# Attention and a feed-forward layer in one kernel: sums of squares, weight scales and masks made by other engines, under a new order of steps

## Chip, cores and metric

One core of one Trainium2 chip runs the whole program. The metric is the device time of one execution in microseconds. TensorE does the matmuls, VectorE, ScalarE and GpSimd the element work, SyncE (SP) issues loads and transposing transfers. Every engine and every queue runs its own instructions in the order in which they were written, and waits for others by semaphores.

## What is computed

```
scores = scale * q @ k.T                       # 8 batches, 8 heads, 576 positions, head size 64
mask   = local (0 <= rel < 32) for heads 0-3;  strided (rel >= 0, same position mod 32) for heads 4-7
attn   = softmax(where(mask, scores, -1e9)) @ v
x      = attn, laid out as 4608 tokens x 512
h      = x @ w_in                              # 512 x 1024
solu   = h * softmax(h)
ln     = (solu - mean) / sqrt(var + 1e-6) * g_ln
out    = ln @ w_out                            # 1024 x 512
```

`w_in` and `w_out` arrive as 64-bit floats and are decoded on the chip.

## The kernel before

**Precision.** TensorE multiplies 16-bit floats. A 32-bit operand is split into a high part (a rounded copy, written by ScalarE) and a low part (the remainder, written by VectorE), and a product is made as three matmuls: high x high, high x low, low x high. So that the parts fit, each operand is scaled by a power of two taken from its sum of squares: `pow2_scale` (lines 320 to 351) adds the partial sums over the partitions with a matmul against ones (L330), takes half the exponent as the root (L340), and makes the scale and its reciprocal by three small VectorE steps (L343 to L346).

**Attention.** For each batch there are four units (`unit`, from line 460): two of the strided heads (6 and 5 blocks, called half 1 in the code) and two of the local heads. A unit fills its scores with the mask (for batch 0 a matmul with the unit matrix, L505, later a ScalarE copy, L496), adds q k (L514), takes the maximum (L522), subtracts it (for batch 0's units by a matmul, L527, with the exponent behind it, L531), sums (L532, L545), inverts the sum (L549, L550), and scales by it on GpSimd (L553). For batch 0 the result is turned by TensorE (L565) and scaled on the way back by ScalarE with `one`, the reciprocal of the value scale (L568); later batches are split and turned by a transposing transfer (L580). Then come the product with the values (L607), and the split of the result into the ring of tokens, `xs` for strided and `xl` for local heads: high part by ScalarE (L628), low part by VectorE (L629).

**Values.** `v_scale` (line 390) finds the scale of a batch's values. It squares them on ScalarE with an accumulator (L410, two instructions for a batch), sums, and makes the scale; `hscale` (L418) combines it with the scale of `w_in`. There is a second way in the code, for batches named in `V_PE`: TensorE multiplies the upper halves of the values with themselves in blocks of 128 columns, and VectorE takes the diagonal. `V_PE` is empty. `v_split` (line 437) splits the values of batches 1 to 7 into high and low (L443, L444) and has three transfers shift the local ones by 32 rows into `ve` (L457); for batch 0 TensorE makes the shifted copy in three pieces (`load_first_v`, L377 and L378).

**Weights.** `prep_w` (line 796) loads `w_in` in four chunks of 128 rows, decodes each (`decode`: ScalarE L787, GpSimd L792, VectorE L793), takes the diagonal of its gram (L806, L809), makes one scale for all four, and then splits each chunk (L814 on ScalarE, L815 on VectorE). `prep_o` does the like for `w_out`.

**Feed-forward.** `ff(n)` handles 128 tokens: 24 matmuls of 512 columns with `w_in` (L671 to L673), two maxima (L677), exponent (L681), product and sums (L683), mean and squares (L687, L688), norms on GpSimd, split (L728, L729), a transposing transfer, 24 matmuls with `w_out` (L745 to L747), and the store (L755).

**Masks** are one loaded array of 128 x 3 x 96 (L277), from which GpSimd makes a copy for the strided units (L266) and the local ones (L272 to L274).

**Order.** The kernel doesn't issue as it goes. `Plan.add` collects 1576 steps, each with its engine, a planned duration and what it reads and writes. `ORDER` is a written-out list of step numbers, and the steps are issued in it. Filler matmuls on ones (L257), 56 of them, keep TensorE running at the start: 12 at first, `WARM` = 16 pairs and, later, `LATE` = 6 pairs.

Of the kernel before, what the change touches and what calls it, by code (L numbers as in the profile page):

```python
# [9 lines left out]
BF16 = mybir.dt.bfloat16  # L10
# [3 lines left out]
ALU = mybir.AluOpType  # L14
# [5 lines left out]
STRIDE = 32  # L20
# [40 lines left out]
V_PE = ()  # L61
# [4 lines left out]
47 1 3-5 29 27 22 28 39 21 2 82 34 6-8 48 23 49 20 30-31 40 50 35 42 53 9-11 36 32 105-106 89 107-108 41 37 90 109 91  # L66
38 83 92 110 12 54 13 93 44 59-60 94 0 45 84-85 33 123 55 124 51 140 56 25 86 147 14 65 95 125 139 61 111 43 148 62
126-127 149 15 52 16 87 17 57 18 172 150 112 19 98 141 26 58 96 66-67 296 63 151 68 295 128 64 99 142 69-70 152 71-72
97 73 143-144 80 129 100 113 88 173 114 153 103 81 174 177 299 101 116 74 115 117 332 76 104 175 165 24 102 187 166 75
178 300-301 118 132 167 302 154 77 315 179 130 121 46 119 316 120 131 78 133 331 155 189 188 122 168 145 169 317 182  # L70
170 303 134 318 137 338 180 138 158 135 485 156 159 79 136 190 157 339 304 297 176 305-306 184 171 319 487 215 320 340
181 183 307 341 321 354 185 342 355 160 333 216-217 343-344 163 322 161 486 357 186 345 164 218-220 346 191-192 162
193 235 194 222 195 356 308 221 196 201 358 309 298 359 223 199 237 334 363 224 323 310 207 236 211 213 364 238-239
200 225 240 212 324 255 241 365 546 226-227 311 242 366 313 257 325 312 491 347 492 314 335 229 488 326 256 243 337
203 258-260 230 197 244 493 329 262 261 275 198 494 327 245 507 263 330 328 205 277 204 246 336 202 348 367 349 264
352 508 278 231 209 232 247 276 248 350 509 279 265 523 280 524 656 353 249 210 547 208 206 282 351 549 380 655 250
495 251 510 368 530 369 360 281 228 266 548 233 283 146 370 531 284 511 532 382 533 371 550 401 267 372 381 234 534
269 383 214 551 555 512 285 379 535 384 270 373 286 556 513 385 557 496-497 287 252 657 253 498 387 694 536 558 499
559 489 661 388 386 268 374 500 402-403 490 422 404 514 289 377 405 375 378 376 290 254 406 515 658 693 501 389 502
271 503 407 423 505 662 408 424 409 504 392 410 425-426 390 537 413 361 443 291 560 552 391 847 516 272 525 663 393  # L80
517 288 411 664 444 395 427 412 396 428-429 273 506 414 677 445 397 430 526 518 716 561 274 416 446-447 415 678 665
538 553 539 679 448 417 519 850 394 450 521 455 464 562 540 431 680 700 719 434 432 449 563 529 522 292 666 717 293
520 701 294 433 451 527 466 564 528 702 667 703 718 452 465 541 720 453 398 467 435 704 399 542 668 468 543 681 469
721 682 544 437 436 545 669 454 722-723 438 683-684 471 725 849 362 470 685 400 456-457 565 848 571 472 726 473-475
573 418 659 458 727 592 885 705 566 728 572 853-854 574 439 554 670 567 419 476 459 575 660 671 420 855 706 1017 729
569 576 707 477 568 570 577 593 695 578 594 856 886 421 869 696 579 672 580 857 908 595 673 870 613 708 440 674 698
# [80 lines left out]
def attn_solu_kernel(ctx: ExitStack, tc: tile.TileContext, qloc, qstr, kloc, kstr, vloc, vstr, w_in, w_out, g, masks, out):  # L167
# [780 lines left out]
```

## Time and profile before

| | |
|---|---|
| time, median of 3 runs | 483.84 us (481.33 to 484.36) |
| the profiled execution: time, span | 482.54 us, 480.6 us |
| TensorE busy | 467.7 us (97%) |
| ScalarE, VectorE, GpSimd busy | 350.2, 323.3, 175.8 us |
| loads, first 30 us | 366 GB/s |
| first feed-forward matmul starts at | 45.63 us |

The span goes from the first to the last instruction; the time of a run is longer by what lies around it. A wait is the idle time of an engine just before an instruction, put down to what ended it. An idle engine costs time only if it is the one that sets the end in that stretch.

### The profile page before, as it was taken

How to read it: one execution, taken by the hardware profiler on the slowest of the kernel's cores; microseconds unless marked ns; L12 is line 12 of the kernel's file. 1: busy time of each engine (PE TensorE's matmuls, PEld its weight loads, DVE VectorE, ACT ScalarE, POOL GpSimd, SP SyncE). 2: the span in 40 equal slices, each digit the busy share in tenths (PEclk: the TensorE clock that was granted, in tenths of full speed). 3: DMA queues.
4: the chain of work that ended last, by engine and by line, in shares of the span. 5: the costliest groups of instructions: out<-in, count | busy, mean ns of one | idle time of the engine just before them, and what ended most of it. 6: DMA issues, size and time to landing. Idle time of an engine off the chain costs nothing.

```text
span 480.6 us, 15173 instructions
## 1 busy us (share of the span) xinstructions
PE 467.7 (97%) x6484; PEld 238.9 (50%) x6484; DVE 323.3 (67%) x699; ACT 350.2 (73%) x569; POOL 175.8 (37%) x328
## 2 busy tenths in 40 slices
PE   9988899999899999999999999999999999999997
PEld 3765455554455454545554454455454445444444
DVE  1599999989759867878686667655754764435440
ACT  3499999999787996787798677966664664564661
POOL 4533525476333423152414413422331723112420
PEclk9989999999999999999999999999999999999999
DMA  8997699698959997697759945575651794233353
GB/s 335 420 369 287 203 195 303 150 157 201 208 136 284 185 223 187 114 263 117 181 191 221 203 85 125 113 184 123 132 101 34 120 178 89 64 88 71 78 113 95
DMA packets 131555, 83.21 MB, mean 173 GB/s; under 512 B 117376, under 2 KB 118208, under 8 KB 130976
## 3 DMA queue, kind: packets, MB, share of 16 engines
q1 hardware_dynamic: 126304, 72.88, 65.2%
q10 hardware_dynamic: 5184, 9.37, 5.7%
q8 instruction: 50, 0.82, 0.7%
q14 instruction: 17, 0.14, 0.1%
HBM read 39.24 MB, written 9.44 MB: 101 GB/s over the span
## 4 chain that ended last, share of the span: by engine, by line
PE 85%; ACT 4%; DVE 4%; DMA 4%; issue 2%; SPq 1%; ACTq 0%; DVEq 0%
PE h_ps L671 12%; PE o_ps L745 11%; PE o_ps L746 11%; PE o_ps L747 11%; PE h_ps L672 11%; PE h_ps L673 11%; PE x_ps L607 4%; PE s_ps L514 4%; DMA ve<-vl 2%; PE o_ps L257 2%; DMA raw<-w_out 1%; ACT vs L410 1%; DVE st L677 1%; ACT raw L681 1%; DVE m L545 1%
## 5 line engine op out<-in xcount | busy, mean ns | idle before, releaser
L745 PE MATMUL o_ps<-ohi,cc 128*128 128x512 f16 x272 | 103.3, 380 | 0.0
L746 PE MATMUL o_ps<-obuf,cc 128*128 128x512 f16 x272 | 103.2, 379 | 0.0
L747 PE MATMUL o_ps<-ohi,cc 128*128 128x512 f16 x272 | 103.2, 379 | 0.0
L677 DVE TENSOR_REDUCE st<-h_ps 128x1 f32<-128x512 f32 x70 | 47.2, 686 | 50.6 <-PE h_ps L673 50.3
L683 DVE SCALAR_TENSOR_TENSOR raw<-h_ps,raw 128x512 f32<-128x512 f32 x70 | 47.4, 685 | 27.8 <-ACT raw L681 27.0
L681 ACT ACTIVATE raw<-h_ps,st,vsc 128x512 f32<-128x512 f32 x62 | 48.0, 775 | 24.8 <-DVE st L679 22.5
L553 POOL TENSOR_TENSOR t<-t,m 128x648 f32<-128x648 f32 (+5 forms) x32 | 40.9, 1279 | 64.7 <-DVE m L550 54.2
L729 DVE SCALAR_TENSOR_TENSOR cc<-raw,st,cc 128x1024 f16<-128x1024 f32 (+1 forms) x38 | 46.4, 1226 | 15.1 <-ACT cc L728 14.9
L671 PE MATMUL h_ps<-w,xl 128*128 128x512 f16 x140 | 53.3, 381 | 1.4 <-issue 0.9
L687 ACT ACTIVATE raw<-raw,st 128x1024 f32<-128x1024 f32 x36 | 41.2, 1147 | 17.5 <-DVE st L686 16.6
L671 PE MATMUL h_ps<-w,xs 128*128 128x512 f16 x140 | 53.1, 379 | 0.0
L672 PE MATMUL h_ps<-w,xs 128*128 128x512 f16 x140 | 53.1, 379 | 0.0
L673 PE MATMUL h_ps<-w,xs 128*128 128x512 f16 x140 | 53.1, 379 | 0.0
L673 PE MATMUL h_ps<-w,xl 128*128 128x512 f16 x140 | 53.1, 379 | 0.0
L672 PE MATMUL h_ps<-w,xl 128*128 128x512 f16 x140 | 53.1, 379 | 0.0
L728 ACT ACTIVATE cc<-raw,st 128x1024 f16<-128x1024 f32 (+1 forms) x38 | 41.6, 1100 | 13.1 <-POOL st L718 11.0
L747 PEld LDWEIGHTS <-cc 128*128 128x128 f16 x296 | 28.9, 98 | 33.6
L745 PEld LDWEIGHTS <-cc 128*128 128x128 f16 x296 | 28.9, 98 | 32.8 <-DMA cc<-cc 0.3
L746 PEld LDWEIGHTS <-cc 128*128 128x128 f16 x296 | 29.0, 98 | 31.8
L755 ACT ACTIVATE ob<-o_ps,st 128x512 f32<-128x512 f32 x34 | 23.3, 686 | 29.0 <-PE o_ps L747 25.9
L691 POOL TENSOR_SCALAR st<-st 128x1 f32<-128x1 f32 x36 | 14.9, 414 | 76.6 <-ACT raw L681 74.7
L716 POOL TENSOR_SCALAR st<-st 128x1 f32<-128x1 f32 x32 | 6.2, 194 | 97.6 <-ACT raw L688 96.8
(197 smaller groups left out, 889.8 us busy)
## 6 DMA issues: line engine op xcount, KB each, us to landing
out<-ob ACTq DMA_DIRECT2D x35, 256.0 KB, 2.3
q<-qstr SPq DMA_DIRECT2D x8, 594.0 KB, 5.3
k<-kstr SPq DMA_DIRECT2D x8, 594.0 KB, 5.5
q<-qloc SPq DMA_DIRECT2D x8, 576.0 KB, 5.2
k<-kloc SPq DMA_DIRECT2D x8, 576.0 KB, 5.3
raw<-w_in SPq DMA_DIRECT2D x4, 1024.0 KB, 15.3
ve<-vl SPq DMA_DIRECT2D x7, 480.0 KB, 5.5
vrs<-vstr SPq DMA_DIRECT2D x4, 768.0 KB, 6.4
```

Of the source, the lines that this page charges most:

```text
L671: nc.tensor.matmul(hv[i], xhi[cc], whi[:, cc, cols], start=(cc == 0), stop=False)
L672: nc.tensor.matmul(hv[i], xhi[cc], wlo[:, cc, cols], start=False, stop=False)
L673: nc.tensor.matmul(hv[i], xlo[cc], whi[:, cc, cols], start=False, stop=(cc == 3))
L677: add("dve", 0.69, lambda i=i: nc.vector.tensor_reduce((nm, nm2)[i], hv[i], axis=AX.X, op=ALU.max, negate=True), r=[HH[i]], w=[(ST, "nm", i)])
L681: add("act", 0.73, lambda i=i, q=q: nc.scalar.activation(e[:, parts2[i]], hv[i], AF.Exp, bias=nm, scale=hs, accum_out=q), r=[HH[i], (ST, " ...
L683: add("dve", 0.7, lambda i=i, x=x: nc.vector.scalar_tensor_tensor(u[:, parts2[i]], hv[i], 1.0, e[:, parts2[i]], op0=ALU.mult, op1=ALU.mult ...
L687: add("act", 1.13, lambda: nc.scalar.activation(u, u, AF.Identity, bias=mean), r=[(U, 0), (U, 1), (ST, "mean")], w=[(U, 0), (U, 1)])
L728: add("act", w / 1200 + 0.295, lambda cols=cols: nc.scalar.mul(c[:, 0, cols], u[:, cols], r), r=[(U, 0), (U, 1), (ST, "r")], w=CC[0][mine])
L729: add("dve", w / 980 + 0.23, lambda cols=cols: nc.vector.scalar_tensor_tensor(c[:, 1, cols], u[:, cols], r, c[:, 0, cols], op0=ALU.mult, o ...
L745: nc.tensor.matmul(dst, ct[:, cc, :], ohi[:, cc, cols], start=(cc == 0), stop=False)
L746: nc.tensor.matmul(dst, ct[:, cc, :], olo[:, cc, cols], start=False, stop=False)
L747: nc.tensor.matmul(dst, ct[:, 8 + cc, :], ohi[:, cc, cols], start=False, stop=(cc == 7))
```

## The change

Four things change, and the list of steps with them (1581 now).

`V_PE` is (0, 1): the values of batches 0 and 1 go by TensorE's grams, ten matmuls for the local and twelve for the strided values of each, instead of ScalarE's squares.

The input weights are scaled by halves: chunks 0 and 1 have one scale, 2 and 3 another (the rows of the first half meet the local heads, those of the second the strided heads). A step `common` takes the larger scale, and `rho` is each half's share of it. It goes into the value scales, one for each half of the heads (`hscale` has a third instruction), and for batch 0's strided units into the split of the result, whose low part is now one instruction for each block of a pair.

The masks are not loaded. GpSimd writes zeros and then affine selects put -8e9 where nothing may pass: four for the strided mask, ten for the local one.

The order is another throughout. At the start: SP loads q and local values before k, then chunks 2 and 1 of `w_in`, then q and k of the local heads, then chunks 0 and 3, then batch 0's strided values; batch 1's values come behind the second chunk of `w_out` (before, they came ahead of all of `w_out`). GpSimd makes the local mask, then the strided one, ahead of every decode. TensorE issues 22 fillers, one shifted piece, four fillers, both strided score products, and by the fourth gram of `w_in` 38 fillers and one batch's value grams (before, 44 fillers and two transposes). VectorE runs batch 0's value scale, both weight scales, `common` and `hscale` ahead of the first low part of the weights; ScalarE's first high part of the weights stands behind the first decode of `w_out`. Batch 0's last value product and unit 2 of batch 1 stand ahead of the first feed-forward matmul (before, the value product stood between the two halves of that tile).

```diff
-V_PE = ()
+V_PE = (0, 1)
...
-    vsc_sb = buf("vsc", [P, 6], n=4)
-    (mask_sb,) = buf("mask", [P, 3, KL])
+    vsc_sb = buf("vsc", [P, 8], n=4)
+    (mask_sb,) = buf("mask", [P, QS])
...
+    rho = w_sc[:, 10:12]
...
+    def keep(t, pattern, base, by):
+        nc.gpsimd.affine_select(out=t, in_=t, pattern=pattern, compare_op=ALU.is_ge, fill=-8e9, base=base, channel_multiplier=by)
     def mask_strided():
-        nc.gpsimd.tensor_copy(mk_str, mask_sb[:, 2:3, 0:QS].broadcast_to([P, 6, QS]))
+        nc.gpsimd.memset(mask_sb, 0.0)
+        for row in range(0, P, D):
+            m = mask_sb[row : row + D].rearrange("p (g j) -> p g j", j=NI)
+            keep(m, [[-NI, RS], [-1, NI]], 0, 1)
+            keep(m, [[NI, RS], [0, NI]], NI - 1, -1)
+        nc.gpsimd.tensor_copy(mk_str, mask_sb.unsqueeze(1).broadcast_to([P, 6, QS]))
     def mask_local():
-        m = mask_sb
+        near = mk_loc[:, 1, 0]
+        nc.gpsimd.memset(near, 0.0)
         for row in range(0, P, STRIDE):
...
+            keep(near[rows], [[1, KW]], -1, -1)
+            keep(near[rows], [[-1, KW]], STRIDE, 1)
+        nc.gpsimd.tensor_copy(mk_loc[:, 1, 1:6], mk_loc[:, 1, 0:1].broadcast_to([P, 5, KW]))
+        nc.gpsimd.tensor_copy(mk_loc[:, 0], mk_loc[:, 1])
+        for row in range(0, P, QL):
+            keep(mk_loc[row : row + STRIDE, 0, 0], [[1, KW]], -STRIDE, 0)
     def load_masks():
-        add("sp", 0.4, lambda: nc.sync.dma_start(mask_sb, masks), w=["mask_raw"])
...
         def hscale():
-            nc.vector.tensor_scalar(sc[:, 2:3], sc[:, 0:1], w_sc[:, 0:1], None, op0=ALU.mult)
+            nc.vector.tensor_scalar(sc[:, 2:3], sc[:, 0:1], w_sc[:, 8:9], None, op0=ALU.mult)
             nc.vector.reciprocal(sc[:, 4:5], sc[:, 2:3])
+            nc.vector.tensor_scalar(sc[:, 6:8], rho, sc[:, 1:2] if b else sc[:, 5:6], None, op0=ALU.mult)
...
-        add("act", w / 1266 + 0.354, lambda: nc.scalar.mul(hi, vr, sc[:, 1:2]), r=[("vr", a, raw), ("vsc", b % 4)], w=V[:1])
+        add("act", w / 1266 + 0.354, lambda: nc.scalar.mul(hi, vr, sc[:, 6 + a : 7 + a]), r=[("vr", a, raw), ("hsc", b % 4)], w=V[:1])
...
+            one, ONE = (vsc_sb[0][:, 5:6], "one") if half else (vsc_sb[0][:, 6:7], ("hsc", 0))
...
+            if b == 0 and half:
+                def low(src=src, dh=dh, dl=dl, k=k):
+                    for j in range(k):
+                        nc.vector.scalar_tensor_tensor(dl[:, j], src[:, j], rho[:, 1:2], dh[:, j], op0=ALU.mult, op1=ALU.subtract)
+                add("act", w / 1200 + 0.17, lambda src=src, dh=dh: nc.scalar.mul(dh, src, rho[:, 1:2]), r=[X[y], "w_sc"], w=H)
+                add("dve", w / 960 + 0.09 + 0.11 * k, low, r=[X[y], "w_sc", *H], w=L)
+                continue
...
-        for cc in range(4):
-            decode(stage[cc], ...)
+        for half in (0, 1):
+            mine = (2 * half, 2 * half + 1)
+            for cc in mine:
+                decode(stage[cc], ...)
...
-        pow2_scale(w_sc, [w_sc[:, 4 + cc : 5 + cc] for cc in range(4)], ...)
+            own = w_sc[:, 2 * half : 2 * half + 2]
+            pow2_scale(own, [w_sc[:, 4 + cc : 5 + cc] for cc in mine], ...)
...
+        def common():
+            nc.vector.tensor_scalar(w_sc[:, 8:9], w_sc[:, 0:1], w_sc[:, 2:3], None, op0=ALU.max)
+            nc.vector.reciprocal(w_sc[:, 9:10], w_sc[:, 8:9])
+            nc.vector.tensor_scalar(rho, w_sc[:, 0:4:2], w_sc[:, 9:10], None, op0=ALU.mult)
```

## Rows read from the trace of the kernel before

**Rows 1.** Page, busy time: engine, us, share of the span, instructions

```profile
PE 467.7 (97%) x6484; PEld 238.9 (50%) x6484; DVE 323.3 (67%) x699; ACT 350.2 (73%) x569; POOL 175.8 (37%) x328
```

**Rows 2.** Busy time by stretch: from:to, length, busy of each engine, clock, DMA, GB/s

```profile
0.00:30.00 30.00, 28.36 (x365) 16.04 (x366) 13.38 (x38) 14.83 (x22) 15.34 (x34) 1.00 0.92 366
30.00:60.00 30.00, 25.69 (x508) 16.73 (x508) 29.18 (x64) 29.06 (x47) 13.71 (x11) 0.94 0.76 280
60.00:100.00 40.00, 40.00 (x795) 21.17 (x794) 38.49 (x85) 39.51 (x66) 19.08 (x31) 1.00 0.86 207
```

**Rows 3.** Waits of TensorE: waiting <- releaser: us in total, times, longest

```profile
PE x_ps L607 <- DMA ve<-vl: 1.8, 1, 1.8
PE s_ps L514 <- ACT s_ps L496: 1.6, 2, 0.9
PE o_ps L330 <- DVE diag L834: 1.3, 1, 1.3
PE o_ps L257 <- DVE ones L253: 1.1, 1, 1.1
```

**Rows 4.** Busy time by stretch, the last 10.6 us

```profile
470.00:480.60 10.60, 7.05 (x57) 4.28 (x55) 0.35 (x1) 1.27 (x2) 0.00 (x0) 0.95 0.26 71
```

**Rows 5.** Busy time by stretch, of line L257 alone: matmul, weight load, clock, DMA

```profile
0.00:57.00 57.00, 15.82 (x56) 5.80 (x56) 0.97 0.84 333
```

**Rows 6.** Timeline, 14 to 56 us: start, length, engine, line, operation [wait before]

```profile
14.10 0.79 DVE L522 TENSOR_REDUCE m<-h_ps 128x5 f32<-128x270 f32 x2 [3.07 <-PE h_ps L514]
...
25.65 1.12 POOL L792 TENSOR_SCALAR raw<-raw 128x1024 int32<-128x1024 uint8 x1 [1.89 <-DMA raw<-w_in]
...
28.13 1.08 PE L806 MATMUL x_ps<-cc 128*128 128x128 bf16 x16
...
45.40 1.21 DVE L793 SCALAR_TENSOR_TENSOR obuf<-obuf,raw 128x1024 int32<-128x1024 int32 x1
...
45.63 0.38 PE L671 MATMUL h_ps<-w,xl 128*128 128x512 f16 x1
...
55.29 0.19 PE L330 MATMUL o_ps<-o_sc,ones 128*128 128x1 bf16 x2 [1.30 <-DVE diag L834]
```

**Rows 7.** Groups by line, ScalarE, 0 to 31 us: busy, mean ns | idle before

```profile
L410 ACT ACTIVATE vs<-vs 128x1536 f16<-128x1536 f32 x1 | 1.5, 1475 | 0.0
L410 ACT ACTIVATE vs<-vrl 128x1280 f16<-128x1280 f32 x1 | 1.3, 1262 | 0.0
L410 ACT ACTIVATION_READ_ACCUMULATOR vs<-vs 128x1 f32 x1 | 0.2, 193 | 0.0
```

**Rows 8.** Groups by line, VectorE, 27.1 to 46.62 us

```profile
L629 DVE TENSOR_TENSOR xs<-x_ps,xs 128x324 f16<-128x324 f32 (+1 forms) x4 | 1.8, 462 | 0.1
...
L809 DVE SCALAR_TENSOR_TENSOR diag<-x_ps,unit 128x128 bf16<-128x128 f32 x3 | 0.8, 271 | 0.3 <-PE x_ps L806 0.2
...
L809 DVE DVE_READ_ACCUMULATOR diag<-x_ps,unit 128x1 f32 x3 | 0.3, 84 | 0.0
...
L344 DVE RECIPROCAL w_sc<-w_sc 128x1 f32<-128x1 f32 x1 | 0.2, 165 | 0.0
...
L346 DVE TENSOR_SCALAR w_sc<-w_sc 128x1 f32<-128x1 f32 x1 | 0.2, 154 | 0.0
```

**Rows 9.** Busy time of TensorE by stretch, with the granted clock

```profile
30.00:32.00 2.00, 1.22 (x51) 1.00 1.04 422
32.00:34.00 2.00, 2.00 (x10) 0.58 1.01 410
34.00:36.00 2.00, 2.00 (x58) 0.56 1.04 422
```

**Rows 10.** Chain that ended last, in order of time: start, length, engine, line

```profile
7.68 0.86 PE x_ps L377 x2
8.54 0.97 PE x_ps L378 x2
```

**Rows 11.** Groups by line, GpSimd, 0 to 15 us

```profile
L273 POOL CAST mk_loc<-mask 32x384 bf16<-32x384 f32 x4 | 3.1, 770 | 0.0
L272 POOL CAST mk_loc<-mask 32x64 bf16<-32x64 f32 x4 | 0.9, 230 | 0.1
...
L315 POOL TENSOR_SCALAR_AFFINE_SELECT ident<-ident 128x128 f32<-128x128 f32 x1 | 0.3, 292 | 0.1
```

More of the change, by code (lines that the diff above doesn't have):

```diff
@@ L124 @@
+1550 1571 1575 1573-1574 1577 1579 1524 1580 1576 1578
 """
@@ L232, in attn_solu_kernel @@
     whi, wlo = w16[:, :, 0, :], w16[:, :, 1, :]
-    (w_sc,) = buf("w_sc", [P, 8])
+    (w_sc,) = buf("w_sc", [P, 12])
     (diag,) = buf("diag", [P, P], BF16)
@@ L799, in prep_w @@
         ST = [[("c", i, y, a) for y in range(2) for a in range(2)] for i in range(2)] + CT[:2]
-        for cc in range(4):
-            decode(stage[cc], w_in[cc * P : (cc + 1) * P, :].rearrange("p (a f) -> p a f", a=2), cc, ST[cc], ROOMS[cc], W_SHIFT)
-            def gram(cc=cc):
-                x = stage[cc].bitcast(BF16).rearrange("p (f t) -> p f t", t=2)[:, :, 1]
-                for i in range(8):
-                    nc.tensor.matmul(wg_ps[cc], x[:, i * P : i * P + P], x[:, i * P : i * P + P], start=(i == 0), stop=(i == 7))
-            add("pe", 0.6, gram, r=ST[cc], w=[("x", cc % 2)])
-            add("dve", 0.3, lambda cc=cc: nc.vector.scalar_tensor_tensor(diag, wg_ps[cc], 1.0, unit_sb, op0=ALU.mult, op1=ALU.mult, accum_out=w_sc[:, 4 + cc : 5 + cc]),
-                r=[("x", cc % 2), "unit"], w=[("wm", cc)])
@@ L812, in prep_w, with gram @@
[L812 to L817 removed]
+        for half in (0, 1):
+            mine = (2 * half, 2 * half + 1)
+            for cc in mine:
+                decode(stage[cc], w_in[cc * P : (cc + 1) * P, :].rearrange("p (a f) -> p a f", a=2), cc, ST[cc], ROOMS[cc], W_SHIFT)
+                def gram(cc=cc):
+                    x = stage[cc].bitcast(BF16).rearrange("p (f t) -> p f t", t=2)[:, :, 1]
+                    for i in range(8):
+                        nc.tensor.matmul(wg_ps[cc], x[:, i * P : i * P + P], x[:, i * P : i * P + P], start=(i == 0), stop=(i == 7))
+                add("pe", 0.6, gram, r=ST[cc], w=[("x", cc % 2)])
+                add("dve", 0.3, lambda cc=cc: nc.vector.scalar_tensor_tensor(diag, wg_ps[cc], 1.0, unit_sb, op0=ALU.mult, op1=ALU.mult, accum_out=w_sc[:, 4 + cc : 5 + cc]),
+                    r=[("x", cc % 2), "unit"], w=[("wm", cc)])
+            own = w_sc[:, 2 * half : 2 * half + 2]
+            pow2_scale(own, [w_sc[:, 4 + cc : 5 + cc] for cc in mine], [("wm", cc) for cc in mine], ("w_sc", half), (wg_ps[mine[1]][:, 0:1], ("x", 1)), mul=2.0**W_SHIFT, shift=0, floor=2.0**-64)
+            for cc in mine:
+                add("act", 1.13, lambda cc=cc, own=own: nc.scalar.mul(whi[:, cc], stage[cc], own[:, 1:2]), r=[("w_sc", half), *ST[cc]], w=[("wh", cc)])
+                add("dve", 1.28, lambda cc=cc, own=own: nc.vector.scalar_tensor_tensor(wlo[:, cc], stage[cc], own[:, 1:2], whi[:, cc], op0=ALU.mult, op1=ALU.subtract),
+                    r=[("w_sc", half), ("wh", cc), *ST[cc]], w=[("w", cc)], lock=True)
```

141 lines of the change are left out of this document (66 added, 75 removed).

## The prediction

> **What bounds the kernel now.** I read the page's engine table first, then busy time by stretch, then TensorE's waits, and only then the timeline of the first 60 us. TensorE is busy 467.7 of 480.6 us [rows 1], so 12.9 us of the span are not matmul. By stretch [rows 2] TensorE is filled without a gap from 60 to 100 us, while from 30 to 60 us VectorE (29.18 of 30) and ScalarE (29.06) are the full ones and TensorE is not: the start is bounded by the vector engines, the rest by TensorE. The listed waits [rows 3] put 1.8 us on one late copy of shifted values near 131 us, 1.6 us on mask copies, 1.3 us on the output weights' scale, 1.1 us on the very first memset; the others are under 1 us each. After the last matmul 10.60 - 7.05 = 3.55 us of store are left [rows 4]. So the memset and the store (4.65 us) stay whatever the order is, and 8.2 us of waits can be changed. In the first 57 us TensorE also runs 56 filler matmuls, 15.8 us busy [rows 5]; the change keeps all 56, since WARM and LATE stand.
>
> **The change part by part.** The profiled execution took 482.54 us for a span of 480.6, so 1.9 us lie around the span; the median of the runs is 483.84, 1.3 us above it. I sum against 480.6.
>
> TensorE. Two batches' values are squared by grams: (10 + 12) x 2 = 44 matmuls of 128x128, priced by the 16 grams of the input weights that took 1.08 us [rows 6], so 0.065 us each, 2.8 us in all with one more scale product. Nothing leaves TensorE. The span can therefore not fall below 467.7 + 2.8 + 4.65 = 475.2, a time of 477.1, and only if every other wait goes.
>
> ScalarE. Four squares leave: 1.26 to 1.48 us each plus 0.19 us for the accumulator [rows 7], 6.2 us. On the path they count nothing by themselves: ScalarE's steps of the start feed VectorE's (high part before low part, exponent before sum), and VectorE has no slack there.
>
> VectorE only gains work. Two diagonals of 0.27 + 0.08 [rows 8] make 0.7; a second scale of the input weights (root and three small steps at 0.15 to 0.17 each [rows 8]) 0.66; the common factor, three such steps, 0.5; a third step in hscale, 0.3 for the two batches; the low parts of batch 0's strided half go from 4 instructions to 11 pieces of 108 columns. The last is between nothing and 11 x 0.27 - 1.8 = 1.1 us; I take 0.9, because the nearest row is a 128-column scalar_tensor_tensor out of PSUM (0.27). Together 3.1 us before the first feed-forward tile; later hscale's step, six times 0.15 us, lies beside TensorE's full stretches.
>
> Loads. SP issues no mask load, and the input weights' loads move ahead of vstr of batch 0 and ahead of both value loads of batch 1. By the arrays' sizes, 8.6 MB were asked for up to and with the last input chunk before, 7.1 MB now; at the 0.366 MB per us of the first 30 us [rows 2] that is 4 us earlier than its arrival at 25.65 [rows 6]. Batch 1's values queue behind two output-weight chunks; their grams stand so far down TensorE's order that this is hidden (estimate: landed by 34 us, wanted near 39).
>
> Does the earlier data help? The new order says little. The new first-half scale could start the weights' split early, but ScalarE's first high part stands behind an output-weight decode and VectorE's first low part behind both scales, the common factor and hscale. TensorE's queue up to the fourth input gram has 6 fillers less (-1.2 us), two transposes less (-0.7), 22 value grams more (+1.4) and a scale product more (+0.15): -0.35 us. Before, that gram ended at 28.13 + 1.08 = 29.2 with 0.5 us of waits behind it [rows 6]; so now 28.3 without any wait, and 29.0 is what I take, since this queue still has to wait for VectorE's maxima and decodes. The earlier chunk thus buys 0.2 to 0.9 us, not 4.
>
> From there VectorE decides. Before, it needed from 29.2 to 45.40 + 1.21 = 46.6 us [rows 6] to have all four weight splits, batch 0's first three units and three output-weight decodes behind it: 17.4 us with almost no gap. The new list to that point: 17.4, less the last unit's sum and reciprocal, now ahead of it (1.3), plus batch 0's value scale, now behind it (0.7), plus the added work without what falls ahead (3.1 - 0.5 = 2.6), plus batch 1's hscale, which is now ahead of a weight split (0.4): 19.8. From 29.0 that gives 48.8, **2.2 us later**. Ends: 28.3 and no cost of the pieces, 47.2 (+0.6); one more hand-over of 1.3 us such as the one at the output scale [rows 3], 50.1 (+3.5). Everything behind (output scale at 55.29 [rows 6], first tiles) hangs on the same VectorE queue and moves with it; the remaining TensorE work there is the same.
>
> The body. The step of unit 2 of batch 2 that waited 1.8 us for the shifted copy has its three copies issued ahead of that unit's transpose now, where all three stood behind it. The gain is 0 to 1.8 us; new waits of an order never seen can cost as much. I take -0.9.
>
> [...]
>
> Sum: 480.6 + 2.2 - 0.9 = 481.9, with 1.9 around it **483.8**, rounded to 484: even with the median.
>
> **The rivals.**
> *Faster: TensorE's waits go.* For it: data comes 4 us earlier, ScalarE has 6.2 us less, and a held clock would be worth up to 43% of the 4 us from 32 to 36, 1.7 us. If VectorE, whose first maximum moves from 14.1 [rows 6] to about 11.7 (one shifted piece of 0.86 + 0.97 us [rows 10] and four fillers fewer ahead of it, one block more in the product), never waited, the start would be +0.6, the copy -1.8, the output scale -1.3, the clock -1.7: 476.4 + 1.9 = 478.3. Against it: VectorE's longer list. Chance 0.12.
>
> *Slower: GpSimd's masks come late.* The masks were loaded; now a memset, 14 affine selects (8 and 2 for the local mask, 4 for the strided one) and copies make them, and the local mask, wanted second, stands first in GpSimd's queue. Its setup ends near 3 us; memsets and copies are some 2 us. The first score product wants the strided mask at 10.4 (22 fillers, one shifted piece, four fillers). At 0.29 us, the row of a 128x128 select [rows 11], it is ready at 9.1; at 0.23, the row of a 32x64 copy, earlier. At 0.77, the mean of the 32x384 copies, at 15.8: 5.4 us late, of which VectorE's idle time takes some 2, giving 483.8 + 3.4 = 487.2; at 1.0 us a select 490. It decides from about 0.5 us on. I take 0.29, for it is the same operation. Chance 0.12.
>
> *Slower: new waits behind 60 us.* VectorE has 38.49 of 40 and ScalarE 39.51 of 40 from 60 to 100 us [rows 2]; an order that lets output-weight splits fall behind the first second product would stop TensorE for some us: 484 + 4 to 6, 489. TensorE had none there before. Chance 0.1.
>
> *The change does not do what it says*, in that halves and freed ScalarE time change nothing because of the order, is the forecast itself: chance 0.66, own range 481 to 487.
>
> **How the numbers follow.** A change under 1% (4.8 us) can hardly be told from none here. Faster by more than that needs 479.0 or less, within 2 us of TensorE's floor: 0.12. Slower needs 488.7: the two slow rivals, each for most of its chance, 0.19 with the forecast's tail. Same: 0.69. The range leaves out about a tenth on each side: 479 to 489, the floor's neighbourhood below and late masks or new waits above.
>
> **What would show it.** Right: the last input chunk lands near 21, the fourth input gram still ends near 29, VectorE is full from there, and the first feed-forward matmul starts at 47 to 50 with batch 0's last value product behind it. Wrong: that matmul starts before 45.6, or VectorE idles between 30 and 48, or the first score product waits for GpSimd, or waits of over 1 us on TensorE appear behind 60 us.

## The result and the profile after

The changed kernel takes 485.02 us (median of 11 runs, 484.71 to 488.89), the kernel before, run beside it, 482.88 (11 runs, 481.18 to 484.36). The ratio is 1.0058 with a 95% interval from 1.0041 to 1.0075: slower by 0.6%, within the 1% of "same" and within the range given. The profiled execution took 484.71 us for a span of 483.0, so the span grew by 2.4 us where the forecast's sum was +1.3.

The page's busy time, to be held against [rows 1]: TensorE has 4.3 us more, VectorE 7.0 more, ScalarE 4.1 less.

```profile
PE 472.0 (98%) x6526; PEld 242.8 (50%) x6526; DVE 330.3 (68%) x725; ACT 346.1 (72%) x561; POOL 178.0 (37%) x337
```

Busy time by stretch, as [rows 2] and [rows 9] (length, busy of each engine, clock, DMA share, GB/s):

```profile
0.00:30.00 30.00, 28.57 (x372) 16.15 (x373) 14.76 (x38) 11.13 (x15) 16.41 (x43) 1.00 0.89 354
30.00:60.00 30.00, 26.15 (x529) 18.16 (x527) 29.21 (x76) 24.99 (x38) 11.78 (x10) 0.94 0.80 265
60.00:100.00 40.00, 38.43 (x711) 19.87 (x712) 38.17 (x83) 37.58 (x62) 19.62 (x26) 1.00 0.76 191
36.00:38.00 2.00, 0.82 (x12) 0.44 (x14) 2.00 (x8) 1.89 (x4) 0.00 (x0) 0.91 0.29 54
38.00:40.00 2.00, 2.00 (x43) 1.40 (x40) 1.97 (x3) 1.06 (x3) 0.00 (x0) 0.50 0.92 375
40.00:42.00 2.00, 2.00 (x18) 1.10 (x18) 2.00 (x7) 2.00 (x3) 0.60 (x1) 0.74 1.01 374
```

From 30 to 60 us VectorE is as full as before while ScalarE now has 5 us to spare: of the two engines that were full there, VectorE is the one left. The fall of the clock has moved from 32 to 36 us to 38 to 42, again behind idle time of TensorE (1.2 of the 2 us before).

TensorE's waits, as [rows 3] (waiting <- releaser: us in total, times, longest):

```profile
PE o_ps L343 <- DVE diag L866: 2.1, 1, 2.1
PE s_ps L259 <- DVE ones L255: 1.1, 1, 1.1
PE x_ps L622 <- DVE xs L647: 1.1, 1, 1.1
PE s_ps L528 <- issue: 0.9, 1, 0.9
PE s_ps L528 <- ACT s_ps L510: 0.7, 2, 0.4
PE h_ps L695 <- DVE raw L707: 0.5, 2, 0.3
```

The wait for shifted copies is gone, the one at the output scale has grown from 1.3 to 2.1, and a new one stands in front of it: batch 0's second strided value product waits for the pieces of low parts (L647).

The timeline of VectorE, TensorE and GpSimd where [rows 6] stood (start, length, engine, line, operation [wait before]; one fence for each engine, the lines between are left out):

```profile
12.88 0.83 DVE L536 TENSOR_REDUCE m<-s_ps 128x12 f32<-128x648 f32 x1 [10.58 <-PE s_ps L528]
21.48 0.71 DVE L563 TENSOR_SCALAR m<-m 128x10 f32<-128x10 f32 x1
22.35 2.06 DVE L817 SCALAR_TENSOR_TENSOR cc<-cc,raw 128x1024 int32<-128x1024 int32 x1
26.36 1.22 DVE L817 SCALAR_TENSOR_TENSOR cc<-cc,raw 128x1024 int32<-128x1024 int32 x1
32.94 1.02 DVE L434 TENSOR_SCALAR vsc<-w_sc,vsc 128x2 f32<-128x2 f32 x1
36.20 1.51 DVE L647 SCALAR_TENSOR_TENSOR xs<-x_ps,w_sc,xs 128x108 f16<-128x108 f32 x6
40.42 1.27 DVE L647 SCALAR_TENSOR_TENSOR xs<-x_ps,w_sc,xs 128x108 f16<-128x108 f32 x5
41.61 2.06 DVE L841 SCALAR_TENSOR_TENSOR w<-cc,w_sc,w 128x1024 f16<-128x1024 f32 x1
47.50 0.21 DVE L434 TENSOR_SCALAR vsc<-w_sc,vsc 128x2 f32<-128x2 f32 x1
49.17 1.27 DVE L841 SCALAR_TENSOR_TENSOR w<-cc,w_sc,w 128x1024 f16<-128x1024 f32 x1
54.74 1.34 DVE L563 TENSOR_SCALAR m<-m 128x10 f32<-128x10 f32 x1
```
```profile
1.93 6.69 PE L259 MATMUL o_ps<-ones 128*128 128x480 bf16 x20
11.29 0.33 PE L519 MATMUL s_ps<-ob,unit 64*64 64x324 bf16 x4
29.52 0.62 PE L832 MATMUL x_ps<-cc 128*128 128x128 bf16 x8 [0.28 <-DVE w_sc L353]
50.67 0.39 PE L695 MATMUL h_ps<-w,xl 128*128 128x512 f16 x1
59.51 0.19 PE L343 MATMUL o_ps<-o_sc,ones 128*128 128x1 bf16 x2 [2.11 <-DVE diag L866]
```
```profile
19.40 1.16 POOL L816 TENSOR_SCALAR raw<-raw 128x1024 int32<-128x1024 uint8 x1 [5.69 <-DMA raw<-w_in]
22.24 1.10 POOL L816 TENSOR_SCALAR raw<-raw 128x1024 int32<-128x1024 uint8 x1
31.58 2.36 POOL L816 TENSOR_SCALAR raw<-raw 128x1024 int32<-128x1024 uint8 x2
41.40 1.20 POOL L816 TENSOR_SCALAR raw<-raw 128x1024 int32<-128x1024 uint8 x1 [7.10 <-DMA raw<-w_out]
```

Hold the first fence against the third. The decode step of a 128x1024 tile takes 2.06 us at 22.35 and 1.22 at 26.36; the weight split takes 2.06 at 41.61 and 1.27 at 49.17; the two-column step takes 1.02 at 32.94 and 0.21 at 47.50. Each of the three long ones begins while GpSimd's decode step is under way (22.24 to 23.34, 31.58 to 33.94, 41.40 to 42.60). Their excess is 0.8 + 0.8 + 0.8 = 2.4 us. Two small steps of 128x10, whose own time is 0.16, are long as well, beside other GpSimd steps (0.71 at 21.48, 1.34 at 54.74): 0.5 and 1.2 more. In the kernel before, three VectorE rows to 56 us are long in this way, for 0.5 + 0.4 + 0.4 = 1.3 us:

```profile
26.16 0.63 DVE L549 TENSOR_SCALAR m<-m 128x10 f32<-128x10 f32 x1
42.14 1.61 DVE L793 SCALAR_TENSOR_TENSOR obuf<-obuf,raw 128x1024 int32<-128x1024 int32 x1
49.98 0.58 DVE L549 TENSOR_SCALAR m<-m 128x10 f32<-128x10 f32 x1
```

Between the end of the fourth gram and the last weight split the excess is 1.6 us after (32.94 and 41.61) against 0.4 before (42.14). That is what the experiments below follow.

The loss can be placed by the start of the same feed-forward matmul in the two kernels, counted in the order of the program. The first starts 5.0 us later (50.67 against 45.63), the 49th, behind the output scale, 3.5, the end of the span comes 2.4 later. So the start loses 3.5 to 4.2 us and the body gives back about 1.1. In the ledger of the span this is TensorE's busy time +4.3 (the grams 3.2, and 1.1 more for the same 56 fillers, 16.91 against the 15.82 of [rows 5]) and its idle time -1.9.

Of those 1.1 us of the fillers 0.9 lie in the first 22, and they belong to the execution and not to the change. At the start the fillers of 480 columns follow each other every 0.40 us, later every 0.20. That is 1.2 and 2.4 columns a nanosecond, though the granted clock of that stretch is shown as 1.00. In this execution the pace changed 6.7 us into the span, in the one of the kernel before at 5.1, and over all the traces kept here between 4.7 and 7.1. In short_decode and gp_short below, which run the same program up to there, it changed at 4.7: the same 20 fillers took 5.65 and 5.69 us and not 6.69, and the first score product began at 10.26 and 10.29 and not 11.29. TensorE's queue has little room behind it (its waits up to the fourth gram are 1.1 us at the memset and 0.28), so everything up to that gram starts about a microsecond later by it. When the pace changed in the executions without a trace is not known.

The GpSimd groups to 15 us show the masks (busy, mean ns | idle before), against the neighbours in [rows 11]:

```profile
L268 POOL TENSOR_SCALAR_AFFINE_SELECT mk_loc<-mk_loc 32x64 bf16<-32x64 bf16 x10 | 2.3, 232 | 0.6
L268 POOL TENSOR_SCALAR_AFFINE_SELECT mask<-mask 64x54 f32<-64x54 f32 x4 | 1.0, 240 | 0.3
```

### The profile page after: what moved, and what is told of

Same layout as the page of the kernel before. It is cut to its first block, busy times and chain, and to the rows that moved or that the text cites. A ratio compares the mean times of both kernels' runs of the same rounds, so it can differ in the third digit from the quotient of the medians.

```text
span 483.0 us, 15287 instructions
## 1 busy us (share of the span) xinstructions
PE 472.0 (98%) x6526; PEld 242.8 (50%) x6526; DVE 330.3 (68%) x725; ACT 346.1 (72%) x561; POOL 178.0 (37%) x337
## 4 chain that ended last, share of the span: by engine, by line
PE 78%; DVE 10%; ACT 8%; issue 1%; POOL 1%; ACTq 0%; POOLq 0%; DVEq 0%
PE o_ps L769 11%; PE o_ps L770 11%; PE o_ps L771 11%; PE h_ps L695 10%; PE h_ps L696 10%; PE h_ps L697 10%; PE x_ps L622 4%; PE s_ps L528 4%; PE o_ps L259 2%; ACT raw L705 1%; ACT raw L712 1%; DVE st L701 1%; DVE obuf L817 1%; ACT cc L752 1%; DVE w L841 1%
## 5 line engine op out<-in xcount | busy, mean ns | idle before, releaser
L701 DVE TENSOR_REDUCE st<-h_ps 128x1 f32<-128x512 f32 x70 | 47.5, 686 | 47.4 <-PE h_ps L697 47.2
L567 POOL TENSOR_TENSOR t<-t,m 128x648 f32<-128x648 f32 (+5 forms) x32 | 39.4, 1234 | 71.2 <-DVE m L564 57.1
L740 POOL TENSOR_SCALAR st<-st 128x1 f32<-128x1 f32 x32 | 9.1, 284 | 109.4 <-ACT raw L712 108.7
L536 DVE TENSOR_REDUCE m<-s_ps 128x12 f32<-128x648 f32 (+4 forms) x30 | 22.5, 751 | 23.7 <-PE s_ps L528 23.5
```

The lines of the kernel that those rows point to most:

```text
L701: add("dve", 0.69, lambda i=i: nc.vector.tensor_reduce((nm, nm2)[i], hv[i], axis=AX.X, op=ALU.max, negate=True), r=[HH[i]], w=[(ST, "nm", i)])
```

## Experiments

Each was timed beside the kernel before on the same chip, whose median there is named with it. "The k-th matmul" below is the start of that feed-forward matmul, less the start of the same one in the kernel before:

```
us later than before:   1st    49th   121st   481st   961st   end of span
after                  +5.0   +3.5   +5.9    +3.7    +3.8    +2.4
one_gram               +4.0   +2.5   +5.9    +3.5    +4.5    +8.1
thin_grams             +6.4   +7.3   +9.6    +7.4    +7.4    +6.0
short_decode           +1.9   +0.5   +2.9    +0.7    +0.5    -0.9
gp_short               +2.1   +0.6   +2.9    +0.8    +0.7    -0.5
after_lean             +4.3   +3.7   +6.1    +3.9    +3.8    +2.4
gp_quarters            +3.1   +1.8   +4.2    +2.0    +2.8    +1.4
decode_act             +4.4   +3.1   +5.5    +3.3    +3.3    +2.4
copies_first           +0.8   +0.5   +0.6    +1.8    +1.8    +1.9
masks_only             +0.3   +0.2   +0.3    -0.6    -0.7    -0.4
grams_only             +4.9   +5.2   +10.6   +11.5   +15.3   +14.5
```

Each row is one execution. The 1st and 49th columns hold TensorE's pace at the start as well (some 0.8 us of it in after, about none in short_decode and gp_short), and between the columns the new order does other work than the old (the step from the 49th to the 121st is +2.3 to +2.4 in most of its rows). So a row is to be held against the row of after, and not one column against the next.

My theory was that VectorE's longer list sets the start; the first rival that TensorE's grams or the order do.

### Steps and order, crosswise

```
old_steps_new_order: the kernel before, its 1576 steps in the changed kernel's order
new_steps_old_order: the changed kernel, its 1581 steps in the order of before
```

**old_steps_new_order.** 

> The steps of the kernel before (squares by ScalarE, one weight scale, loaded masks) in the new order. Theory VectorE: the added VectorE work (3.1 us) and the grams are gone, the copies of batch 2 stay early: 481.5 to 483 (ratio 0.997 to 1.000), first feed-forward matmul 2 to 3 us earlier than in the changed kernel. Rival order (the new order itself costs the time): 484.5 or more (ratio 1.004 or more).

**new_steps_old_order.** 

> The steps of the changed kernel in the old order, the new steps put where what they replace stood. Theory VectorE: the 3.1 us of VectorE work are added to the old start and the wait for the copies of batch 2 is back: 485.5 to 488 (ratio 1.006 to 1.012). Rival order: the old order with the new steps is about the kernel before, 482.5 to 484 (ratio 1.000 to 1.003).

502.13 us, ratio 1.0381, and 522.41, ratio 1.0822, beside 482.76. The second lies outside what either theory gave. The first lies in the rival's open range (484.5 or more), but 17 us above the changed kernel, so it can't be the share of the order in a loss of 2.4. In the first, TensorE's scores wait 6.6 us for issue and 4.4 for the mask copy; in the second the value product waits for batch splits that now hang on the weights' scale:

```profile
PE x_ps L622 <- ACT vs L457: 7.8, 2, 4.7
PE x_ps L622 <- DMA pt<-p: 5.7, 1, 5.7
```

An order fits only its own steps. These two runs price nothing, and no share of the loss can be given to "the order" by itself.

### Grams, and a stop that was not expected

```diff
 one_gram (after): each value gram a single matmul
-                    n = VW[a] // P
+                    n = 1
 thin_grams (after): all matmuls issued, all but the first of each gram one column wide
+                        c = P if i == 0 else 1
```

**one_gram.** 

> The changed kernel, but each value gram is one matmul instead of ten or twelve (40 of the 44 value grams are left out, so the scale is taken from a part of the squares). TensorE loses 40 x 0.065 = 2.6 to 2.9 us, VectorE nothing. Theory VectorE (the start ends when VectorE's list ends): within 0.7 us of the changed kernel, 484.3 to 485.3 (ratio to before 1.003 to 1.006). Rival TensorE queue (the grams sit in a full queue and each microsecond of them is paid): 482.1 (ratio 0.998).

489.6 us, ratio 1.013 (1.0102 to 1.0159): slower than the changed kernel, which nobody expected. At the start it is 1.0 us ahead of the changed kernel from the first matmul to the 49th; by the 121st a transposing transfer that comes late (a wait of 0.80 at 77.94) has taken that. Of the 1.0, 0.4 is TensorE's earlier pace (5.9 against 6.7 us), so 2.3 us of grams left out give at most 0.6, and VectorE's list from the fourth gram's end to the last weight split is no shorter (20.6 us against 20.3). Most of the grams' time is not paid. The loss comes later, in the timeline of TensorE and its busy time by stretch (as above) near 365 us:

```profile
363.89 0.81 PE L528 MATMUL s_ps<-k,q 64*32 64x64 f32 x51
367.91 0.46 PE L528 MATMUL s_ps<-k,q 64*32 64x64 f32 x13 [3.21 <-issue]
```
```profile
364.00:366.00 2.00, 0.70 (x51) 0.57 (x52) 0.00 (x0) 0.00 (x0) 0.00 (x0) 1.00 2.13 213
366.00:368.00 2.00, 0.09 (x7) 0.09 (x12) 0.00 (x0) 0.00 (x0) 0.00 (x0) 0.92 0.46 78
368.00:370.00 2.00, 2.00 (x18) 0.74 (x18) 1.45 (x4) 0.00 (x0) 0.00 (x0) 0.50 1.21 273
```

TensorE stops for 3.2 us in the middle of one score product, with nothing to wait for that the profile shows, and runs at the low clock behind it. In that gap the transfers show one packet of 16 KB in the queue for instructions, among two transposing transfers (page section 3 for 364.7 to 367.9 us; packets, MB, share of 16 engines). It lands at 366.55, and TensorE goes on 1.36 us later:

```profile
q1 hardware_dynamic: 1475, 0.37, 128.3%
q8 instruction: 1, 0.02, 1.8%
```

If such packets bring TensorE's program, which is inferred, one that is 80 instructions shorter (40 matmuls with their weight loads) has its pieces end elsewhere. That was tried next.

**thin_grams.** 

> The changed kernel with all 44 value grams still issued, but 40 of them one column wide (the scale of two batches comes out wrong). TensorE's program has as many instructions as in the changed kernel, so every piece of it is fetched at the same place; only the time of the grams is left out. If one_gram lost its 5 us because its program is 80 instructions shorter and a fetch fell into crowded transfers, there is no such stop here, and the time is the changed kernel's or up to 1 us below it: 484 to 485 us. If it lost them by the missing grams themselves (less work to keep the clock, another pace), it loses them again: 488.5 to 490.

485.38 us, ratio 1.0053 (1.0027 to 1.0079), beside 482.58: as the theory of the program's pieces had it, if 0.4 above the span it gave. TensorE works through 355 to 375 us without a gap:

```profile
360.00:365.00 5.00, 5.00 (x25) 2.29 (x24) 3.24 (x5) 3.69 (x6) 1.73 (x3) 1.00 0.04 9
365.00:370.00 5.00, 5.00 (x176) 2.96 (x175) 2.07 (x6) 0.15 (x1) 0.13 (x1) 1.00 1.20 181
```

With the length of the program restored and the gram work still left out, the stop near 365 us is gone: it goes with the length of the program and not with the grams' time. That it lies where a piece ends is inferred. (This profile lost 4 us more than the changed kernel's in the first 60 us, with the clock down twice, at 0.50 to 0.51 from 40 to 44 us and 0.50 from 58 to 60, and with stops of its own put down to issue, 0.78 us at 50.32 and 2.00 at 56.90, which end 1.47 and 1.61 us after a packet landed; its median did not.)

### VectorE's work

```diff
 short_decode (after): VectorE's step of the output weights' decode
-  di, di, 3, w0
+  di[:, :128], di[:, :128], 3, w0[:, :128]     # n >= 4
```

**short_decode.** 

> The changed kernel, but the four VectorE decodes of the output weights cover an eighth of their columns (the low bits of the other columns are left out). VectorE loses 4 x about 1.05 = 4.2 us, all before the output scale; TensorE nothing. Theory VectorE: 2.5 to 4 us faster than the changed kernel, 481 to 482.5 (ratio 0.996 to 0.999), the output scale's wait on TensorE shorter. Rival TensorE queue: no change, 484.5 to 485.5.

482.16 us, ratio 0.9991 (0.9968 to 1.0013): the changed kernel with 2.7 us less of VectorE's work (three steps of 0.28 and one of 1.28, held beside GpSimd at 32.93, where each took 1.21) is 2.9 us faster and level with the kernel before, and the wait at the output scale falls from 2.1 to 0.7. In the profiles the fourth gram ends 1.3 us earlier, ahead of every shortened step; 1.0 of that is TensorE's earlier pace. From there to the last weight split VectorE takes 17.5 us and not 20.3: 1.9 less for two short steps and 0.8 less for the two-column step, which meets no GpSimd step here (0.21 us). So the time hangs on VectorE's list; how much a microsecond of the list is worth can't be read from this run, for the pace differs too.

### VectorE beside GpSimd

```diff
 gp_short (after): GpSimd's step on 128 columns, VectorE reads them eight times
-  nc.gpsimd.tensor_scalar(w0, top, ...)
+  nc.gpsimd.tensor_scalar(w0[:, 0:128], top[:, 0:128], ...)
 after_lean: hscale by single columns; unit 1 takes rho with its value scale
-  tensor_scalar(sc[:, 6:8], rho, ...)
+  for a in range(2): tensor_scalar(sc[:, 6 + a : 7 + a], rho[:, a : a + 1], ...)
-  one, ONE = (vsc_sb[0][:, 5:6], "one") if half else ...
+  one, ONE = (vsc_sb[0][:, 5:6], "one") if n == 0 else (vsc_sb[0][:, 6 + half : 7 + half], ("hsc", 0))
-  if b == 0 and half:                            # low parts in pieces
+  if n == 0:
 decode_act (after_lean): GpSimd's step of the output weights by ScalarE
+  nc.scalar.activation(w0, top, AF.Copy, bias=-15.5 / 32, scale=1.0 / 32)
 gp_quarters (after_lean): GpSimd's step in four pieces
+  for i in range(0, 1024, 256):
```

**gp_short.** 

> The changed kernel with GpSimd's step of all eight weight decodes done for 128 of 1024 columns (about 0.2 us instead of 1.1 to 1.2; VectorE's step reads the 128 columns eight times over, so its own work is as long; the weights come out wrong). VectorE has as much work as before. If VectorE instructions stand still while GpSimd runs beside them (2.06 us instead of 1.27 at 22.35 and 41.61, 1.02 instead of about 0.25 at 32.94), these are back at 1.27 and 0.25 here, the first feed-forward matmul starts 1.5 to 2.4 us earlier than at 50.7, and the time is 482.7 to 483.7 us. If those lengths have another cause, they stay and the time is 484.7 to 485.3.

481.92 us, ratio 0.9992 (0.9975 to 1.0009), beside 482.26: 3.1 us under the changed kernel, more than expected, and level with before. VectorE's long instructions are back at their own length:

```profile
21.41 1.20 DVE L817 SCALAR_TENSOR_TENSOR cc<-cc,raw 128x1024 int32<-128x1024 int32 x1
31.50 0.21 DVE L434 TENSOR_SCALAR vsc<-w_sc,vsc 128x2 f32<-128x2 f32 x1
39.48 1.28 DVE L841 SCALAR_TENSOR_TENSOR w<-cc,w_sc,w 128x1024 f16<-128x1024 f32 x1
46.23 1.29 DVE L841 SCALAR_TENSOR_TENSOR w<-cc,w_sc,w 128x1024 f16<-128x1024 f32 x1
```

From the fourth gram's end to the last weight split VectorE needs 28.7 to 47.5 = 18.8 us, against 30.1 to 50.4 = 20.3 in the changed kernel: 1.5 us less, as the two stretched rows behind the gram (0.8 each) say. The rest of the gain lies ahead of the gram, 1.4 us in the profiles, and is not the standing still: 1.0 of it is TensorE's pace (changed at 4.7 and not 6.7 us), and the gram ended at 28.8 in short_decode too, although one decode took 2.12 there and 1.20 here. GpSimd's own step is also shorter here, so the run is not pure. Small VectorE steps beside other GpSimd steps stay long (0.77 at 20.48, 1.34 at 51.80). GpSimd stands still in its turn, one piece of 128 columns at 39.49 for 2.57 us, where such a piece takes 0.32 by itself. So the rows show the standing still in both directions; by what means the two engines hold each other up, no row shows.

**after_lean.** 

> The changed kernel with less of VectorE's new work at the start: hscale's new two-column step (1.02 us at 32.94, where GpSimd's decode runs beside it) is written as two one-column steps, and unit 1 of batch 0 takes the weights' factor with its value scale, so that its 5 pieces of low parts (1.27 us) become two plain instructions. If VectorE sets the start, 0.7 + 0.4 us less of it bring the first feed-forward matmul from 50.7 to about 49.6 and the time to 483.5 to 484.3. If something else sets it (TensorE, transfers), 484.7 to 485.3.

483.92 us, ratio 1.0028 (1.0009 to 1.0047), beside 482.58: 1.1 us under the changed kernel, as expected. In its profile the start gains 0.7 at the first matmul and nothing behind it, because other instructions now meet GpSimd's steps (1.97 us at 42.02, 2.18 at 48.43). It shows one thing more, by stretch:

```profile
36.00:38.00 2.00, 1.48 (x44) 1.00 (x44) 1.97 (x8) 2.00 (x4) 1.12 (x2) 1.00 0.46 107
38.00:40.00 2.00, 2.00 (x25) 1.17 (x23) 2.00 (x3) 1.51 (x5) 0.00 (x0) 1.00 1.02 418
```

Here the clock never falls, and the 49th matmul starts no earlier than in the changed kernel (+3.7 against +3.5), with VectorE's list to the last weight split as long (20.3 us). So the low clock from 38 to 42 us, with VectorE full beside it, can have cost the changed kernel little, though none of its own runs is without the fall to settle it. For the kernel before the runs do: 42 of them with a mean granted clock of 0.995 to 0.996 have a median of 482.42 us, 40 with 0.999 or 1.0 one of 482.52. The 1.1 us of the median aren't in this profile, whose span is as long as the changed kernel's.

**decode_act.** 

> after_lean with GpSimd's step of the four output-weight decodes given to ScalarE, right behind ScalarE's own step of the same decode. ScalarE has 5 us idle from 30 to 60 us in the changed kernel and gets four steps of 1.1 to 1.2 us. If it is the standing still beside GpSimd that ate the rest of after_lean's gain (VectorE instructions of 1.97 and 2.18 us there, at 42.0 and 48.4), these fall to 1.2 to 1.3, and the time is 482.2 to 483.3 against after_lean's 483.9. If ScalarE is then what sets the start, 485 to 487.

483.14 us, ratio 1.0017 (0.9997 to 1.0036), beside 482.26: in the span given. From 30 to 60 us no VectorE row of a 128x1024 tile is over 1.28 us, and the list from the fourth gram to the last weight split is 19.6 us and not 20.3; one wait for ScalarE takes 1.08 back. A 128x10 step beside another GpSimd step is still 1.34 us long at 54.27.

**gp_quarters.** 

> after_lean with GpSimd's step of every weight decode written as four steps of 256 columns, same work and same result. If a VectorE instruction that stands still beside GpSimd waits for the end of the GpSimd instruction under way, it waits for a quarter of one now (0.3 us and not 0.8): the two long ones of after_lean (1.97 and 2.18 us at 42.0 and 48.4) come down to at most 1.6, and the time to 482.2 to 483.3 against after_lean's 483.9. If GpSimd's pieces in turn stand still behind VectorE's instructions, so that the decode comes late (a piece of 128 columns took 2.57 us at 39.49 in gp_short), 484 to 486.

483.91 us, ratio 1.0022 (1.0001 to 1.0043), beside 483.02: between the two expectations, and no better than after_lean. The long rows come down to 1.50 at most, as the first expectation has it, and the profile starts the feed-forward 1.9 us earlier than the changed kernel's, 1.0 of it by TensorE's earlier pace; but GpSimd's four pieces take 3.64 us at 40.45, where one step took 1.20 in the changed kernel, and the medians show no gain. The cut works in the rows and not in the time.

### The copies issued ahead

```diff
 copies_first: the order of before, steps 527 to 529 ahead of 540
-464 562 540 431 ... 563 529 522 ... 451 527 466 564 528 702
+464 562 527 529 528 540 431 ... 563 522 ... 451 466 564 702
```

**copies_first.** 

> The kernel before with one edit of its order: the three copies of batch 2's shifted values are issued ahead of the transposing transfer of unit 2, as the changed kernel has it. If the 1.8 us that TensorE waited for a shifted copy is a real loss, this gives 1.5 to 1.8 us: 481.0 to 481.3 us against 482.8, and the wait ve<-vl is gone from TensorE's waits. If another wait takes its place (the copies now delay the transposed weights of unit 2), 482.5 to 483.

483.05 us, ratio 1.0004 (0.998 to 1.0027), beside 482.58: no gain. The wait for the copies is gone, and TensorE stops 0.7 us after the same value product began (131.09). The rows are the timeline, the busy time by stretch, and the transfers from 130.65 to 133.2 us:

```profile
133.21 0.28 PE L607 MATMUL x_ps<-pt,vl 64*64 64x32 f16 x12 [1.38 <-issue]
```
```profile
134.00:136.00 2.00, 2.00 (x9) 0.81 (x9) 0.68 (x4) 2.00 (x5) 1.14 (x2) 0.65 0.54 185
136.00:138.00 2.00, 2.00 (x6) 0.66 (x5) 1.49 (x6) 2.00 (x5) 0.00 (x0) 0.50 2.10 223
```
```profile
q8 instruction: 1, 0.02, 2.7%
```

The packet starts at 130.69 and takes 1.10 us; that TensorE came to this piece of its program before it was there is inferred from the place and the releaser, as in one_gram. What speaks for it is an interval: TensorE goes on 1.42 us after the packet's end, and in the traces of this case 21 stops of 0.5 to 3.7 us that are put down to issue end 1.28 to 1.61 us after the end of a 16 KB packet. The only ones that don't are a stop of 0.93 us near 71 to 81 us that seven of the nine traces of the new order have. In the kernel before, the packet ran from 129.83 to 131.10, and the wait for the copies ended at 132.53, 1.43 after it: by that interval this wait had two ends at once, and taking the copies out of it could give nothing. The clock fell behind the new gap. What was late next was, by that, the program.

### Masks alone, grams alone

```diff
 masks_only: the kernel before with the new mask functions, no mask load
 grams_only: the kernel before
-V_PE = ()
+V_PE = (0, 1)
```

**masks_only.** 

> The kernel before, in its own order, with the masks made by GpSimd and no mask load. If the masks are ready in time (the changed kernel's trace has 0.28 us a select), the first score product waits for nothing and the time is 482 to 483 us, the same as before; the wait of 1.6 us of the scores on the mask copies may shrink. If the selects delay GpSimd's decodes (they stand ahead of them), the first weights' decode on GpSimd starts later than before and the time is 484 to 486 us.

482.98 us, ratio 1.0006 (0.9988 to 1.0025), beside 482.58: the masks cost nothing, and save nothing.

**grams_only.** 

> The kernel before, in its own order, with two batches' squares made by TensorE's grams (44 matmuls, 2.8 us by the rows) instead of ScalarE (four squares, 6.2 us), and nothing else of the change. If VectorE sets the start, ScalarE's 6.2 us are worth nothing and VectorE's two diagonals cost 0.7: 482.8 to 484.5. If ScalarE (29.06 of 30 us busy from 30 to 60) sets it, 479 to 481. If TensorE's program, 88 instructions longer, now meets crowded transfers when a piece of it is fetched, 485 or more, with one wait of over 1 us put down to issue.

497.09 us, ratio 1.0278 (1.0236 to 1.0319), beside 482.26. The third expectation, 485 or more with one wait of over 1 us put down to issue, holds, and says too little: there are three such waits (3.68 us at 85.62, 2.18 at 147.74, 1.96 at 297.24), and part of the loss is not of that kind. In the old order the grams push back what stands behind them in TensorE's queue: the fourth input gram ends at 32.9 (before 29.2), the first feed-forward matmul is 4.9 us later. Behind that come the stops put down to issue, the longest of them:

```profile
85.62 0.61 PE L745 MATMUL o_ps<-ohi,cc 128*128 128x512 f16 x1 [3.68 <-issue]
```

ScalarE's 6.2 us bought nothing here either, but with so much else moved the run doesn't test that cleanly.

## Why the prediction was right

**Outcome.** "Same" at 484.0 was forecast; 485.02 came, 0.6% above the kernel before. The likeliest case, in its own range of 481 to 487, is what happened. The two terms were of the right sign; the start was sized too small.

**TensorE.** 2.8 us of grams were forecast, 3.2 came; without 2.3 us of them one_gram gains at most 0.6 at the start, and thin_grams' median is no lower than the changed kernel's, so leaving them out of the path was right in the main.

**ScalarE.** Its 6.2 us were valued at nothing: ScalarE is 5 us idle from 30 to 60 us now, and the start is later all the same.

**VectorE's list, the step that was mis-sized.** The pieces cost 2.78 against 1.85 us, 0.93 for the 0.9 taken. The fourth gram was put at 29.0 (28.3 to 29.0) and ended at 30.1; the list behind it was put at 19.8 us and took 20.3. Together the last weight split ends at 50.4 instead of 48.8, and the output scale stands at 59.51, 4.2 later than before instead of 2.2. The first feed-forward matmul, at 50.67, lies outside the 47 to 50 that were named as the sign of being right.

Of the 1.6 us at the last weight split, 1.1 are the gram's end. The larger part of that is TensorE's late pace in this execution: 0.9 us are there already at the first score product, and in short_decode and gp_short, with the earlier pace, the gram ended at 28.8 and 28.7, as forecast. By that, an estimate, the first feed-forward matmul would have started near 49.7.

The other 0.5 are the list, and there the sum lacked a term: VectorE's steps standing still beside GpSimd's. Behind the gram they are 1.6 us against the old 0.4. Take the 1.6 out, leave the 0.4, and the list is 19.1, so the counted work was sized 0.7 too high, which hid more than half of the missing term. From the split to the output scale such steps cost 1.2 us (54.74) against 0.4. The durations were taken from the old order without asking what each step would run beside. The old order gave the warning in three VectorE rows, and in four of GpSimd (2.31 us at 38.72 for a form that takes 1.47, for one), and I passed over them.

**Loads.** The last input chunk was put near 21. GpSimd took the fourth chunk at 22.24 without a wait for it, and in gp_short waited for it until 21.80. The gain of 0.2 to 0.9 us at the fourth gram did not come in this execution, whose gram ended 0.9 later than before; in short_decode and gp_short it ended 0.3 and 0.5 earlier.

**Masks.** 0.23 us a select against 0.29 taken, the first score product at 11.29 (10.4 forecast, and 10.3 where TensorE's pace came earlier) not waiting for GpSimd; masks_only is level. The rival of late masks fell.

**Copies.** The 1.8 us went, and the body gave back about 1.1 for the 0.9 taken. That the size fits is partly luck: copies_first shows that the same edit alone gives nothing. What it is worth hangs, by the interval seen there (TensorE going on 1.42 us after a packet's end), on where the next piece of the program falls, which the prediction didn't name as what is late next.

**Clock.** It fell 5.3 us later, and after_lean makes it likely that this was worth little. As in [rows 9], it fell behind idle time of TensorE, 1.2 of the 2 us ahead of it. The length of the gap alone doesn't tell which one brings a fall: behind gaps of 2.11 us here (59.51) and 3.0 in after_lean (59.68) there was none, behind 1.38 in copies_first there was. The value grams did not keep the clock by themselves (0.50 from 38 to 40 us). The faster rival's 1.7 us for a held clock are shown by no run: in the kernel before, executions at a mean clock of 0.995 to 0.996 and at 0.999 or 1.0 have medians 0.1 us apart.

**Waits behind 60 us.** None over 1 us, as the forecast's own case had it; that rival fell.

**Open.** When TensorE's pace at the start changes in the executions without a trace, and so how much of the 0.6% it is: the profiled execution, at 484.71, is the fastest of its 11 although its pace changed late, so the pace explains its profile and not the median. Why the changed order lets VectorE meet GpSimd's decodes three times is only in part when the chunks landed: GpSimd waited 7.10 us for the one at 41.40, but the decodes at 22.24 and 31.58 stand right behind GpSimd's scaling of the exponents (20.88 to 22.15, 30.02 to 31.50). How much of gp_short's and short_decode's gain is the missing fall of the clock (no fall in 11 and 10 of their 12 runs) no run separates.

No version beat the kernel before: short_decode and gp_short, both with work left out, are level with it, and decode_act, complete, is 0.2% above (interval -0.03% to 0.36%).

## What to carry to other kernels

When an engine is the bound and a change moves its work in time, don't carry its durations over as they stand: look at which instructions of the other engine they will run beside, and give the excess that a stretched row of the same form shows as a term of its own. Before you compare places of two single profiles, compare how their first rows ran: the same 20 fillers took 5.7 to 6.8 us here, and everything behind moved with them. Taking a wait off TensorE's path pays only if the next thing is there in time: in copies_first a wait of 1.8 us went and a stop of 1.38 us came. Its program is very likely one of those things: 21 stops put down to issue here, some in the middle of one group of matmuls, ended 1.28 to 1.61 us after the end of an instruction packet. Order and steps are one object in such a kernel; undoing either alone prices neither.

## What the runs showed of the hardware

The traces have a queue for instructions (q8) with packets of 16 KB: 50 of them, 0.82 MB, in the kernel before, 51, 0.84 MB, in the changed one. That they bring TensorE's program is inferred. TensorE stopped near such a packet for 3.2 us in one_gram (transposing transfers beside it), 3.7 in grams_only and 1.4 in copies_first, each time with a stretch at 0.50 of the clock behind it; behind a stop of 2.2 us in grams_only (147.74) the clock stayed at 1.00. In 21 stops TensorE went on 1.28 to 1.61 us after the packet's end; that it had come to the piece before the packet was there is inferred from this interval. With the length of the program ahead the stop came and went (3.21 us in one_gram, none from 355 to 375 us in thin_grams): the two, 80 instructions apart, differ by 4.2 us in the median, more than the whole change.

At the start of an execution TensorE's fillers of 480 columns run at 0.40 us each and then at 0.20. The moment of the change lay between 4.7 and 7.1 us in the traces, even for programs that are alike up to there (after 6.7, short_decode 4.7).

Some steps of VectorE and GpSimd took longer where the two ran beside each other: 0.8 us more for a VectorE step of 1.27 or of 0.21 (after, 41.61 and 32.94), 1.2 us more for one of 0.16 (128x10, 54.74), and 2.57 us for a GpSimd step that takes 0.32 by itself (gp_short, 39.49). VectorE's one-column steps were not held: 0.14 to 0.17 us each at 30.12 to 31.25 in the changed kernel, inside a GpSimd step (30.02 to 31.50).
